# Attention, gating mixer and feed-forward on one core: norms placed earlier, root by Newton steps, one split per weight pair

## The chip, the core and the metric

One core of a Trainium2 chip runs the whole program. The metric is device time in microseconds, the median of several executions. Four engines matter here: TensorE (PE) does the matmuls, VectorE (DVE) and ScalarE (ACT) the elementwise work, and SyncE's queue (SP) issues the DMAs. Each executes its instructions in order.

## The reference

Three layers follow one another on 4 sequences of 576 tokens with 512 features, in fp32:

```
attn:  8 heads of 64; heads 0-3 see the last 32 positions, heads 4-7 every 32nd earlier one
h = gelu_tanh(x @ w_in);  u, v = h[:, :512], h[:, 512:]
v_n = (v - mean(v)) / sqrt(var(v) + 1e-6) * g_ln
x   = x + (u * (w_sg @ v_n + b_sg)) @ w_out          # w_sg mixes the 576 tokens
xn  = (x - mean(x)) / sqrt(var(x) + 1e-6) * g_2
out = x + relu(xn @ w_ch1) @ w_ch2                   # 512 -> 2048 -> 512
```

## The kernel before

**Numbers.** A matmul runs in a reduced fp32 format, so every operand is split into a high part (a cast on ACT) and a low part (the difference, on DVE), and every product is three matmuls: low x high, high x low, high x high (`split` L177, `mm3` L202). Some weights arrive as 64-bit floats and are first turned into fp32 by one ACT and two DVE operations (`from_f64` L186).

**First three stages, batch by batch.** For each of the four sequences there are segments v (5 token tiles, then gelu and norm of v), u (8 groups), g (8 groups, the gate) and y (8 groups, output and residual). The attention of the next sequence is placed between the groups of the one before. Each finished row block y goes to DRAM (`y_d`). Hooks put extra work in front of a group: `PREP_AT`, `NORM0_AT` and `PRE_AT` are lists of such places.

**Last stage.** The 2304 tokens are taken in three blocks of 768 (`sc` 0, 1, 2), each as two halves of 384. The first matrix (512 -> 2048) is computed in 8 pairs of 128-column blocks (`pair` L829) by a scheme with 7 block products in place of 8: each product is 6 matmuls, 42 per pair. It needs 7 combinations of the tokens, x0 to x6 (`expand` L751), and 7 combinations of each weight pair (`combine` L634). The results of the second half, `late`, are kept, while the first half goes on into the second matrix (`ch2` L796): 24 matmuls per pair for the pair before. After 8 pairs the second half is done, 12 matmuls for each of 16 blocks, and `leave` (L818) multiplies by the reciprocal root of the variance, adds the residual and stores.

**Weights.** While block 0 runs, the weights of later pairs are prepared: `piece` loads (and converts) a quarter, `combine` forms three further differences and splits them, `second` splits the second matrix's part. `units` lists these steps, and `prepare(n)` does the next n. Some pieces (`PRE`) are converted in earlier batches and kept in DRAM. `keep` stores a finished pair in DRAM, `fetch` loads it again for blocks 1 and 2. Two buffers hold the first matrix's pairs in turn.

**Norm of a block.** `norm` (L711) has six steps: load; mean of half 0 and of half 1 (`col_sum` adds the four feature blocks on DVE and splits, two matmuls with a matrix of ones add over partitions, one DVE operation subtracts); variance of half 0 and half 1 (squares on ACT, adds on DVE, split, two matmuls); then the scale by g on ACT. `rsqrt` (L741) makes the reciprocal root, needed only in `leave`. Within one step the sum and the matmuls that use it follow one another. For block 0 `NORM0_AT` puts the steps into segments g and y of the last batch; for block 1 the steps come after pairs 6 and 7 of block 0, for block 2 after pairs 2 to 7 of block 1 (`NORM_AT` L65). For blocks 1 and 2, the two scratch tiles of `col_sum`, those of `rsqrt` and the result tile of `leave` share one name, o, with two buffers.

**Order.** The written order is a priority. A planner with its own cost figures goes through the program, gives each engine the first instruction whose inputs are ready by those figures, and fixes each engine's order. Memory is given out in pools on two stacks; a pool's tile can be written only when what lay there before is done. `open_a` to `open_d` (L935 to L966) open the last stage's pools at the last batch's v 0, g 0, y 0 and after it.

Of the kernel before, what the change touches and what calls it, by code (L numbers as in the profile page):

```python
# [43 lines left out]
WX = {1: (0, 0), 2: (1, 1), 7: (2, 5), 4: (3, 2), 5: (4, 3), 6: (5, 4), 3: (6, 6)}  # L44
S_ENGINE = lambda nc: nc.vector
# [103 lines left out]
def mixer_kernel(ctx: ExitStack, tc: tile.TileContext, io, out):  # L149
# [484 lines left out]
    def combine(i):  # L634
        stg = big["stg"]
        wf = stg[:, 2048:3072].bitcast(F32).rearrange("p (k f) -> p k f", k=KD)
        s = stg[:, 4096:4864].bitcast(F32).rearrange("p (s k f) -> p s k f", s=3, k=2)
        a11, a21, a12, a22 = wf[:, 0:2, 0:P], wf[:, 0:2, P:2 * P], wf[:, 2:4, 0:P], wf[:, 2:4, P:2 * P]
        tt = S_ENGINE(nc).tensor_tensor
# [4 lines left out]
        w = w1[i] = big["w1", i % 2].tile([P, 2, 7, 2, P], F32R, tag="w1", name=f"w1_{i % 2}")  # L644
        for src, j, m in ((wf[:, :, 0:P], 0, 2), (wf[:, :, P:2 * P], 2, 2), (s.rearrange("p s k f -> p (s k) f"), 4, 3)):
            split(w[:, 0, j:j + m].rearrange("p s k f -> p (s k) f"), w[:, 1, j:j + m].rearrange("p s k f -> p (s k) f"),
                  src)

    def keep(i):
        nc.sync.dma_start(out=w1_d[i], in_=w1[i].rearrange("p a s k f -> p (a s k f)").bitcast(F32))  # L650

    def fetch(i):
        w = w1[i] = big["w1", i % 2].tile([P, 2, 7, 2, P], F32R, tag="w1", name=f"w1_{i % 2}")
        nc.sync.dma_start(out=w.rearrange("p a s k f -> p (a s k f)").bitcast(F32), in_=w1_d[i])

    def second(i):
        f = big["stg"][:, 3072:4096].bitcast(F32)
# [52 lines left out]

    def norm(sc, step, role):  # L711
# [6 lines left out]
        if step in (1, 2):  # L718
            half = step - 1
            cs = slice(half * TH, (half + 1) * TH)  # L720
            sr = col_sum(sc, half, False)
            mean = bank(role, "ps_m")[:, :TH]
            nc.tensor.matmul(mean, lhsT=one, rhs=sr[:, 1, :], start=True, stop=False)
            nc.tensor.matmul(mean, lhsT=one, rhs=sr[:, 0, :], start=False, stop=True)
            nc.vector.scalar_tensor_tensor(
                out=yc[:, :, cs], in0=mean.unsqueeze(1).to_broadcast([P, KD, TH]), scalar=-1.0 / DM,
                in1=yc[:, :, cs], op0=ALU.mult, op1=ALU.add)
        elif step in (3, 4):
            half = step - 3
            sr = col_sum(sc, half, True)  # L730
            o = bank(role, "ps_v2")[:, :TH]
            nc.tensor.matmul(o, lhsT=one, rhs=sr[:, 1, :], start=True, stop=False)
            nc.tensor.matmul(o, lhsT=one, rhs=sr[:, 0, :], start=False, stop=True)
            if half == 0:
                rbs[sc] = big["rb"].tile([P, 2, TH], F32, tag="rb", name="rb", bufs=2)
            nc.scalar.activation(rbs[sc][:, half, :], o, AF.Identity, scale=1.0 / DM, bias=eps)
        else:
            for k in range(KD):
                nc.scalar.activation(yc[:, k, :], yc[:, k, :], AF.Copy, scale=g_2[:, k:k + 1])

    def rsqrt(sc, half):  # L741
        ve = rbs[sc][:, half, :]
        t, r = scratch(1, 0), scratch(1, 1)
# [4 lines left out]
        nc.vector.tensor_scalar(out=t, in0=t, scalar1=-0.5, scalar2=1.5, op0=ALU.mult, op1=ALU.add)
        nc.vector.tensor_tensor(out=ve, in0=r, in1=t, op=ALU.mult)

    def expand(sc, step):  # L751
# [7 lines left out]
        if step == 0:
            put(0, b11)  # L760
            tt(out=b11, in0=b12, in1=b11, op=ALU.subtract)
        elif step == 1:
            put(6, b22)
            tt(out=b12, in0=b22, in1=b12, op=ALU.subtract)
        elif step == 2:
            tt(out=b22, in0=b22, in1=b11, op=ALU.subtract)
            put(4, b22)
        elif step == 3:
            put(1, b21)
            tt(out=b21, in0=b22, in1=b21, op=ALU.subtract)  # L770
        elif step == 4:
            put(5, b12)
        elif step == 5:
            put(2, b21)
        else:
            put(3, b11)
# [158 lines left out]
    def open_a():  # L935
        close("at")
        right("wst")
        right(("w1", 0))
        big["stg"] = big["wst"].tile([P, 4864], U32, tag="stg", name="stg")

    def open_b():
        close("win")
        right(("w1", 1))
        right(("w2", 0))
# [73 lines left out]
```

## Time and profile before

| | us |
|---|---|
| median of 3 runs | 697.91 (697.89 to 699.45) |
| the profiled execution | 699.26 |
| its span | 697.5 |
| PE busy | 672.5 (96%) |
| DVE busy | 474.0 (68%) |
| ACT busy | 319.0 (46%) |
| mean granted clock of PE | 0.985 |

The page gives busy time per engine and, in 40 slices, how busy each was. The views used below list one engine's instructions in order of time, with the idle time before one and what ended it, or the busy time of every engine in a stretch. The last stage's matmuls begin at 298.7 us.

### The profile page before, as it was taken

How to read it: one execution, taken by the hardware profiler on the slowest of the kernel's cores; microseconds unless marked ns; L12 is line 12 of the kernel's file. 1: busy time of each engine (PE TensorE's matmuls, PEld its weight loads, DVE VectorE, ACT ScalarE, POOL GpSimd, SP SyncE). 2: the span in 40 equal slices, each digit the busy share in tenths (PEclk: the TensorE clock that was granted, in tenths of full speed). 3: DMA queues.
4: the chain of work that ended last, by engine and by line, in shares of the span. 5: the costliest groups of instructions: out<-in, count | busy, mean ns of one | idle time of the engine just before them, and what ended most of it. 6: DMA issues, size and time to landing. Idle time of an engine off the chain costs nothing.

```text
span 697.5 us, 12744 instructions
## 1 busy us (share of the span) xinstructions
PE 672.5 (96%) x5050; PEld 642.9 (92%) x5050; DVE 474.0 (68%) x992; ACT 319.0 (46%) x803; POOL 21.0 (3%) x24
## 2 busy tenths in 40 slices
PE   5899999999999999989999969999999999999997
PEld 4779979989898989979999969999999999999997
DVE  4889787586758685999998885644679347333433
ACT  3888967283568445655454553112434222111121
POOL 0011011000200020000000000000000000000000
PEclk9899999999999999999999979999999999999999
DMA  8863233457431565337867714354335415353001
GB/s 267 274 188 126 84 98 111 150 161 220 150 110 47 194 223 178 125 136 281 306 243 260 283 45 136 92 209 168 151 129 220 149 57 209 121 209 108 22 25 45
DMA packets 34539, 110.05 MB, mean 158 GB/s; under 512 B 3696, under 2 KB 13936, under 8 KB 31408
## 3 DMA queue, kind: packets, MB, share of 16 engines
q1 hardware_dynamic: 34480, 109.25, 46.1%
q8 instruction: 39, 0.64, 0.4%
q14 instruction: 20, 0.16, 0.1%
HBM read 82.76 MB, written 26.48 MB: 157 GB/s over the span
## 4 chain that ended last, share of the span: by engine, by line
PE 75%; DVE 10%; ACT 8%; DMA 5%; issue 1%; SPq 1%; ACTq 0%; DVEq 0%
PE ps_p L783 21%; PE ps_o L205 9%; PE ps_o L204 8%; PE ps_o L203 8%; PE ps_u L203 2%; PE ps_u L205 2%; PE ps_u L204 2%; PE ps_v L203 2%; PE ps_v L204 2%; PE ps_v L205 2%; PE ps_y L203 2%; PE ps_y L205 2%; PE ps_y L204 2%; ACT pt L400 2%; PE ps_t L439 1%
## 5 line engine op out<-in xcount | busy, mean ns | idle before, releaser
L783 PE MATMUL ps_p<-x,w 128*128 128x384 f32 x1008 | 188.2, 339 | 6.2 <-DVE o L821 3.1
L783 PEld LDWEIGHTS ps_p<-x,w 128*128 128x128 f32 x1008 | 177.3, 190 | 9.4 <-DVE o L821 3.4
L204 PE MATMUL ps_o<-h,w 128*128 128x384 f32 x384 | 129.7, 338 | 0.0
L205 PE MATMUL ps_o<-h,w 128*128 128x384 f32 x384 | 129.4, 338 | 0.0
L203 PE MATMUL ps_o<-h,w 128*128 128x384 f32 x384 | 128.6, 336 | 0.0
L205 PEld LDWEIGHTS ps_o<-h,w 128*128 128x128 f32 x384 | 73.3, 191 | 0.0
L204 PEld LDWEIGHTS ps_o<-h,w 128*128 128x128 f32 x384 | 73.1, 190 | 0.1
L203 PEld LDWEIGHTS ps_o<-h,w 128*128 128x128 f32 x384 | 72.6, 189 | 0.2
L789 DVE SCALAR_TENSOR_TENSOR h<-late,h 128x384 fp32r<-128x384 f32 x48 | 26.5, 558 | 47.4 <-ACT h L788 47.4
L788 ACT ACTIVATE h<-late 128x384 fp32r<-128x384 f32 x48 | 25.2, 525 | 68.0 <-PE ps_o L205 68.0
L203 PE MATMUL ps_g<-wsg,vn 128*128 128x288 f32 x128 | 39.0, 305 | 0.0
L205 PE MATMUL ps_g<-wsg,vn 128*128 128x288 f32 x128 | 38.2, 299 | 0.0
L203 PE MATMUL ps_u<-xhl,winl 128*128 128x288 f32 x128 | 38.1, 297 | 0.0
L203 PE MATMUL ps_y<-gt,wout 128*128 128x288 f32 x128 | 37.9, 298 | 0.0
L204 PE MATMUL ps_g<-wsg,vn 128*128 128x288 f32 x128 | 37.9, 296 | 0.0
L204 PE MATMUL ps_u<-xhl,winh 128*128 128x288 f32 x128 | 37.8, 295 | 0.0
L205 PE MATMUL ps_u<-xhl,winh 128*128 128x288 f32 x128 | 37.7, 295 | 0.0
L205 PE MATMUL ps_y<-gt,wout 128*128 128x288 f32 x128 | 37.6, 295 | 0.0
L204 PE MATMUL ps_y<-gt,wout 128*128 128x288 f32 x128 | 37.5, 294 | 0.0
L788 ACT ACTIVATE h<-c 128x384 fp32r<-128x384 f32 x24 | 12.6, 523 | 51.4 <-DVE c L851 51.3
L835 ACT ACTIVATE s<-ps_p 128x384 f32<-128x384 f32 x24 | 11.7, 489 | 49.7 <-PE ps_p L783 49.6
L203 PE MATMUL ps_v<-winh,xhl 128*128 128x512 f32 x80 | 32.2, 403 | 0.2 <-DVE xhl L495 0.2
(183 smaller groups left out, 1328.0 us busy)
## 6 DMA issues: line engine op xcount, KB each, us to landing
w<-w_scratch SPq DMA_DIRECT2D x16, 1792.0 KB, 7.4
w_scratch<-w SPq DMA_DIRECT2D x8, 1792.0 KB, 7.3
stg<-in_w_ch SPq DMA_DIRECT2D x23, 512.0 KB, 5.9
qk<-in_qk_s SPq DMA_DIRECT2D x8, 601.0 KB, 4.3
raw_p<-in_w_ch SPq DMA_DIRECT2D x18, 256.0 KB, 3.1
y_scratch<-y SPq DMA_DIRECT2D x16, 288.0 KB, 2.8
yc<-y_scratch SPq DMA_DIRECT2D x3, 1536.0 KB, 6.9
qk<-in_qk_l SPq DMA_DIRECT2D x7, 592.0 KB, 5.0
```

Of the source, the lines that this page charges most:

```text
L203: nc.tensor.matmul(ps, lhsT=ll, rhs=rh, start=first, stop=False)
L204: nc.tensor.matmul(ps, lhsT=lh, rhs=rl, start=False, stop=False)
L205: last_mm[0] = nc.tensor.matmul(ps, lhsT=lh, rhs=rh, start=False, stop=last)
L400: exps.append(nc.scalar.activation(p3[:, i, :], src, AF.Exp, scale=SCALE, bias=mx[:, i:i + 1], accum_out=sm[:, i:i + 1]))
L439: nc.tensor.transpose(ps[:rows, (t - t0) * c:(t - t0 + 1) * c], src, ident)
L783: nc.tensor.matmul(o, lhsT=w[:, a, wj, k, :], rhs=x[:, c, k, :], start=first and k == 0 and n == 0, stop=k == 1 and n == 2, skip_group_che ...
L788: nc.scalar.activation(h[:, 0, :], src, AF.Relu)
L789: nc.vector.scalar_tensor_tensor(out=h[:, 1, :], in0=src, scalar=0.0, in1=h[:, 0, :], op0=ALU.max, op1=ALU.subtract)
L835: nc.scalar.activation(s1, a, AF.Copy)
```

## The change

The first block's norm moves from the last batch's g and y segments into v and u, its expansion into g and y; the memory for it is opened at v 0 and that of the first weight pair later, at g 0. Each norm step now ends with the column sum of the next step, whose matmuls come one step later; steps for block 1 go after pairs 3 to 6 of block 0 and into the middle of pairs (4.5, 5.5, 6.5). The root starts from ACT's Abs_reciprocal_sqrt and takes two Newton steps in place of Sqrt, reciprocal and one step. A weight pair's 14 blocks lie side by side and are split in one operation each on ACT and DVE. The list of weight steps is reordered, one more piece is converted early, and 13 of the steps instead of 12 are done ahead of the last stage.

```
-PREP_AT = (("u", 2, 2), ("u", 6, 1), ("g", 2, 2), ("g", 4, 1), ("g", 5, 2), ("y", 2, 1), ("y", 4, 2), ("y", 6, 1))
-NORM0_AT = (("g", 0, "n", 0), ("g", 3, "n", 1), ("g", 4, "n", 2), ("g", 6, "n", 3), ("g", 7, "n", 4), ("y", 1, "n", 5),
-            ("y", 2, "e", 0), ("y", 2, "e", 1), ("y", 3, "e", 2), ("y", 4, "e", 3), ("y", 5, "e", 4), ("y", 6, "e", 5),
-            ("y", 7, "e", 6))
-NORM_AT = ({6: (0, 1), 7: (2, 3, 4, 5)}, {2: (0,), 3: (1,), 4: (2,), 5: (3,), 6: (4,), 7: (5,)})
+PREP_AT = (("v", 1, 1), ("v", 3, 1), ("u", 2, 1), ("u", 4, 1), ("g", 1, 1), ("g", 2, 1), ("g", 3, 1), ("g", 4, 1),
+           ("y", 2, 1), ("y", 6, 1), ("y", 7, 1))
+NORM0_AT = (("v", 0, "n", 0), ("v", 4, "n", 1), ("u", 2, "n", 2), ("u", 4, "n", 3), ("u", 6, "n", 4), ("g", 0, "n", 5),
+            ("g", 5, "e", 0), ("g", 7, "e", 1), ("y", 0, "e", 2), ("y", 1, "e", 3), ("y", 2, "e", 4), ("y", 3, "e", 5),
+            ("y", 5, "e", 6))
+NORM_AT = ({3: (0,), 4.5: (1,), 5: (2,), 5.5: (3,), 6: (4,), 6.5: (5,)}, {2: (0,), 3: (1,), 4: (2,), 5: (3,), 6: (4,), 6.5: (5,)})
-PRE = (8, 9, 12, 13, 16, 17, 20, 21, 24)
+PRE = (8, 9, 12, 13, 16, 17, 20, 21, 24, 25)
...
     def combine(i):
         stg = big["stg"]
...
+        c = stg[:, 3072:4864].bitcast(F32)
...
-        for src, j, m in ((wf[:, :, 0:P], 0, 2), (wf[:, :, P:2 * P], 2, 2), (s.rearrange("p s k f -> p (s k) f"), 4, 3)):
-            split(w[:, 0, j:j + m].rearrange("p s k f -> p (s k) f"), w[:, 1, j:j + m].rearrange("p s k f -> p (s k) f"),
-                  src)
+        split(w[:, 0].rearrange("p n f -> p (n f)"), w[:, 1].rearrange("p n f -> p (n f)"), c)
...
-    units = [(fn, a) for i in range(NW) for fn, a in (
-        (piece, (i, 0)), (piece, (i, 1)), (combine, (i,)), (piece, (i, 2)), (piece, (i, 3)), (second, (i,)))]
+    units = [(piece, (0, 0)), (piece, (0, 1)), (piece, (0, 2)), (piece, (0, 3)), (combine, (0,))]
+    for i in range(NW):
+        if i:
+            units += [(piece, (i, 2)), (piece, (i, 3))]
+        if i + 1 < NW:
+            units += [(piece, (i + 1, 0)), (piece, (i + 1, 1))]
+        units += [(second, (i,))]
+        if i + 1 < NW:
+            units += [(combine, (i + 1,))]
...
+        if 1 < step < 6:
+            half = step % 2
             cs = slice(half * TH, (half + 1) * TH)
+            sr = srs.pop(sc)
+            o = bank(role, "ps_m")[:, :TH]
             nc.tensor.matmul(o, lhsT=one, rhs=sr[:, 1, :], start=True, stop=False)
             nc.tensor.matmul(o, lhsT=one, rhs=sr[:, 0, :], start=False, stop=True)
+            if step < 4:
+                nc.vector.scalar_tensor_tensor(
+                    out=yc[:, :, cs], in0=o.unsqueeze(1).to_broadcast([P, KD, TH]), scalar=-1.0 / DM,
+                    in1=yc[:, :, cs], op0=ALU.mult, op1=ALU.add)
+            else:
+                if half == 0:
+                    rbs[sc] = big["rb"].tile([P, 2, TH], F32, tag="rb", name="rb", bufs=2)
+                nc.scalar.activation(rbs[sc][:, half, :], o, AF.Identity, scale=1.0 / DM, bias=eps)
+        if step < 5:
+            srs[sc] = col_sum(sc, (step - 1) % 2, step > 2)
         else:
             for k in range(KD):
                 nc.scalar.activation(yc[:, k, :], yc[:, k, :], AF.Copy, scale=g_2[:, k:k + 1])
...
-        nc.scalar.activation(t, ve, AF.Sqrt)
-        nc.vector.reciprocal(r, t)
-        nc.scalar.activation(t, r, AF.Square)
-        nc.vector.tensor_tensor(out=t, in0=t, in1=ve, op=ALU.mult)
-        nc.vector.tensor_scalar(out=t, in0=t, scalar1=-0.5, scalar2=1.5, op0=ALU.mult, op1=ALU.add)
-        nc.vector.tensor_tensor(out=ve, in0=r, in1=t, op=ALU.mult)
+        nc.scalar.activation(r, ve, AF.Abs_reciprocal_sqrt)
+        for step in range(2):
+            nc.scalar.activation(t, r, AF.Square)
+            nc.vector.tensor_tensor(out=t, in0=t, in1=ve, op=ALU.mult)
+            nc.vector.tensor_scalar(out=t, in0=t, scalar1=-0.5, scalar2=1.5, op0=ALU.mult, op1=ALU.add)
+            nc.vector.tensor_tensor(out=ve if step else r, in0=r, in1=t, op=ALU.mult)
...
+        what = ((0, "t1", 6, "t3"), ("t2", 4), (1, "t4"), (5,), (2,), (3,), ())
+        if sc == 0:
+            what = ((0, "t1"), ("t2", 4), (1, "t4"), ("t3", 5), (2,), (3,), (6,))
...
         if i:
             ch2(sc, 0, f1 - 2, 1 - role)
+        mid()                      # norm steps of i - 0.5
         e = bank(role, "ps_p4")[:, :TH]
...
     def open_a():
         close("at")
         right("wst")
-        right(("w1", 0))
+        right("nm")
+        right("sr")
+        right("rb")
+        big["norm", 0] = big["nm"].tile([P, KD * TC + 2 * TH], F32, tag="n0", name="n0")
         big["stg"] = big["wst"].tile([P, 4864], U32, tag="stg", name="stg")
     def open_b():
         close("win")
+        right(("w1", 0))
         right(("w1", 1))
         right(("w2", 0))
-        right(("w2", 1))
...
+        right(("x", 0))            # x0 and x4
     def open_c():
         close("mid")
-        right("x")
+        right(("x", 1))            # the other five
+        right(("w2", 1))
         right(("w2", 2))
...
-    prepare(max(0, 12 - done[0]))
+    prepare(max(0, 13 - done[0]))
```

## Rows read from the trace of the kernel before

**Rows 1.** The page: busy time of the engines, and the group of products.
```profile
PE 672.5 (96%) x5050; PEld 642.9 (92%) x5050; DVE 474.0 (68%) x992; ACT 319.0 (46%) x803; POOL 21.0 (3%) x24
L783 PE MATMUL ps_p<-x,w 128*128 128x384 f32 x1008 | 188.2, 339 | 6.2 <-DVE o L821 3.1
```
**Rows 2.** Windows: stretch, length, busy time by engine, PE clock, DMA share, GB/s.
```profile
240.00:298.70 58.70, 58.34 (x394) 55.64 (x393) 46.62 (x95) 33.09 (x61) 6.22 (x5) 1.00 0.53 190
298.70:308.50 9.80, 7.60 (x33) 6.26 (x31) 9.80 (x15) 6.22 (x10) 0.00 (x0) 0.83 0.05 16
308.50:396.50 88.00, 87.65 (x501) 86.85 (x502) 81.45 (x150) 41.81 (x71) 0.00 (x0) 1.00 0.78 274
396.50:418.30 21.80, 15.67 (x63) 13.98 (x62) 17.01 (x26) 14.80 (x25) 0.00 (x0) 0.77 0.27 104
510.00:545.00 35.00, 35.00 (x203) 34.91 (x202) 31.38 (x48) 13.81 (x23) 0.00 (x0) 1.00 0.52 186
298.70:690.36 391.66, 382.98 (x2162) 378.79 (x2161) 245.88 (x428) 128.82 (x228) 0.00 (x0) 0.98 0.44 157
```
**Rows 3.** The chain that ended last: 30 undisturbed matmuls (start, length).
```profile
333.31 5.20 PE ps_p L783 x30
```
**Rows 4.** PE's timeline at the stage's head: start, length, instruction, idle before.
```profile
300.42 0.45 PE L783 MATMUL ps_p<-x,w 128*128 128x384 f32 x1 [0.51 <-ACT x L179]
302.02 5.94 PE L783 MATMUL ps_p<-x,w 128*128 128x384 f32 x23 [1.16 <-ACT x L179]
```
**Rows 5.** PE's timeline at the change from block 0 to block 1.
```profile
397.61 0.45 PE L732 MATMUL ps_v<-sr,one 128*128 128x384 f32 x1 [0.74 <-DVE sr L180]
...
403.21 0.44 PE L732 MATMUL ps_v<-sr,one 128*128 128x384 f32 x1 [1.75 <-DVE sr L180]
...
412.34 2.29 PE L783 MATMUL ps_p<-x,w 128*128 128x384 f32 x6 [3.06 <-DVE o L821]
415.21 0.69 PE L783 MATMUL ps_p<-x,w 128*128 128x384 f32 x1 [0.58 <-ACT s L835]
```
**Rows 6.** Timelines of DVE and of SP's queue at the head.
```profile
299.27 0.96 DVE L180 TENSOR_TENSOR x<-n,x 128x768 fp32r<-128x768 f32 x1
300.14 0.95 DVE L766 TENSOR_TENSOR n<-n 128x768 f32<-128x768 f32 x1
...
297.10 10.56 SPq L590 DMA_DIRECT2D y_scratch<-y  x2
```
**Rows 7.** DVE's timeline at the change from block 0 to block 1.
```profile
403.83 2.55 DVE L745 RECIPROCAL o<-o 128x384 f32<-128x384 f32 x1 [0.68 <-ACT o L744]
...
410.39 0.56 DVE L749 TENSOR_TENSOR rb<-o 128x384 f32<-128x384 f32 x1
...
411.73 1.02 DVE L821 TENSOR_TENSOR o<-ps_o,rb 128x384 f32<-128x384 f32 x2
```
**Rows 8.** Timelines of SP's queue and of PE in the last batch.
```profile
246.00 12.54 SPq L188 DMA_DIRECT2D stg<-in_w_ch  x4
269.16 0.38 SPq L715 DMA_DIRECT2D n<-y_scratch  x1
...
279.43 0.44 PE L723 MATMUL ps_m<-sr,one 128*128 128x384 f32 x1 [0.36 <-DVE sr L180]
```
**Rows 9.** DVE: one row of its timeline, then groups (count, busy, mean ns).
```profile
358.02 0.55 DVE L704 TENSOR_TENSOR o<-yc 128x384 f32<-128x384 f32 x1
...
L180 DVE TENSOR_TENSOR w<-stg,w 128x512 fp32r<-128x512 f32 x16 | 10.6, 686 | 0.1
L180 DVE TENSOR_TENSOR w<-stg,w 128x1024 fp32r<-128x1024 f32 x8 | 9.7, 1215 | 6.5 <-ACT w L179 6.5
L748 DVE TENSOR_SCALAR o<-o 128x384 f32<-128x384 f32 x6 | 2.1, 356 | 0.1
```
**Rows 10.** ACT's timeline: the root's table load, and a square.
```profile
323.66 1.28 ACT L744 ACT_TABLE_LOAD   x1
...
282.87 0.51 ACT L701 ACTIVATE n<-n 128x384 f32<-128x384 f32 x1
```

More of the change, by code (lines that the diff above doesn't have):

```diff
@@ L43 @@
 NLATE = 10
[L44 to L45 removed]
+WX = {1: (0, 2, 0), 2: (4, 2, 1), 7: (1, 2, 5), 4: (5, 2, 2), 5: (8, 1, 3), 6: (10, 1, 4), 3: (12, 1, 6)}
 NT = B * S
@@ L623, in piece @@
         stg = big["stg"]
-        w0 = 2048 + 1024 * (j // 2) + WP * (j % 2)
+        w0 = 2048 + 1024 * (1 - j // 2) + WP * (j % 2)
         w = stg[:, w0:w0 + WP]
@@ L635, in combine @@
         stg = big["stg"]
-        wf = stg[:, 2048:3072].bitcast(F32).rearrange("p (k f) -> p k f", k=KD)
-        s = stg[:, 4096:4864].bitcast(F32).rearrange("p (s k f) -> p s k f", s=3, k=2)
+        c = stg[:, 3072:4864].bitcast(F32)
+        wf = c[:, 0:1024].rearrange("p (k f) -> p k f", k=KD)
+        s = c[:, 1024:1792].rearrange("p (s k f) -> p s k f", s=3, k=2)
         a11, a21, a12, a22 = wf[:, 0:2, 0:P], wf[:, 0:2, P:2 * P], wf[:, 2:4, 0:P], wf[:, 2:4, P:2 * P]
-        tt = S_ENGINE(nc).tensor_tensor
+        tt = nc.vector.tensor_tensor
         tt(out=s[:, 0], in0=a21, in1=a22, op=ALU.add)
@@ L643, in combine @@
         tt(out=s[:, 2], in0=a12, in1=s[:, 1], op=ALU.subtract)
[L644 to L647 removed]
+        w = w1[i] = big["w1", i % 2].tile([P, 2, 14, P], F32R, tag="w1", name=f"w1_{i % 2}")
+        split(w[:, 0].rearrange("p n f -> p (n f)"), w[:, 1].rearrange("p n f -> p (n f)"), c)
     def keep(i):
[L650 removed]
+        nc.sync.dma_start(out=w1_d[i], in_=w1[i].rearrange("p a n f -> p (a n f)").bitcast(F32))
     def fetch(i):
[L653 to L654 removed]
+        w = w1[i] = big["w1", i % 2].tile([P, 2, 14, P], F32R, tag="w1", name=f"w1_{i % 2}")
+        nc.sync.dma_start(out=w.rearrange("p a n f -> p (a n f)").bitcast(F32), in_=w1_d[i])
     def second(i):
[L657 removed]
+        f = big["stg"][:, 2048:3072].bitcast(F32)
         w = w2[i] = big["w2", i].tile([P, 2, 2, DM], F32R, name=f"w2_{i}")
         split(w[:, 0].rearrange("p k f -> p (k f)"), w[:, 1].rearrange("p k f -> p (k f)"), f)
[L661 to L662 removed]
+    units = [(piece, (0, 0)), (piece, (0, 1)), (piece, (0, 2)), (piece, (0, 3)), (combine, (0,))]
[7 more added lines that the diff above has]
+            units += [(combine, (i + 1,))]
     done = [0]
@@ L709, in col_sum @@
         return sr
+    srs = {}
     def norm(sc, step, role):
@@ L717, in norm @@
         yc = ys[sc]
-        if step in (1, 2):
-            half = step - 1
+        if 1 < step < 6:
+            half = step % 2
             cs = slice(half * TH, (half + 1) * TH)
[L721 to L731, printed above, removed]
+            sr = srs.pop(sc)
+            o = bank(role, "ps_m")[:, :TH]
             nc.tensor.matmul(o, lhsT=one, rhs=sr[:, 1, :], start=True, stop=False)
             nc.tensor.matmul(o, lhsT=one, rhs=sr[:, 0, :], start=False, stop=True)
-            if half == 0:
-                rbs[sc] = big["rb"].tile([P, 2, TH], F32, tag="rb", name="rb", bufs=2)
-            nc.scalar.activation(rbs[sc][:, half, :], o, AF.Identity, scale=1.0 / DM, bias=eps)
+            if step < 4:
[8 more added lines that the diff above has]
+            srs[sc] = col_sum(sc, (step - 1) % 2, step > 2)
         else:
@@ L756, in put @@
         def put(j, src):
-            x = xns[sc, j] = big["x"].tile([P, 2, 2, TH], F32R, tag=f"x{j}", name=f"x{j}")
+            pl = big["x", 0 if j in (0, 4) else 1]
+            x = xns[sc, j] = pl.tile([P, 2, 2, TH], F32R, tag=f"x{j}", name=f"x{j}")
             split(x[:, 0], x[:, 1], src)
[L759 to L776, printed above, removed]
+        t2 = b22 if sc else big["norm", 0][:, KD * TC:].rearrange("p (k t) -> p k t", k=2)
+        what = ((0, "t1", 6, "t3"), ("t2", 4), (1, "t4"), (5,), (2,), (3,), ())
+        if sc == 0:
+            what = ((0, "t1"), ("t2", 4), (1, "t4"), ("t3", 5), (2,), (3,), (6,))
+        for w in what[step]:
+            if w == "t1":
+                tt(out=b11, in0=b12, in1=b11, op=ALU.subtract)
+            elif w == "t2":
+                tt(out=t2, in0=b22, in1=b11, op=ALU.subtract)
+            elif w == "t3":
+                tt(out=b12, in0=b22, in1=b12, op=ALU.subtract)
+            elif w == "t4":
+                tt(out=b21, in0=t2, in1=b21, op=ALU.subtract)
+            else:
+                put(w, {0: b11, 1: b21, 2: b21, 3: b11, 4: t2, 5: b12, 6: b22}[w])
     def product(sc, i, o, m, first):
-        wj, xj = WX[m]
+        n0, nk, xj = WX[m]
         w, x = w1[i], xns[sc, xj]
@@ L782, in product @@
             for n, (a, c) in enumerate(((1, 0), (0, 1), (0, 0))):
-                nc.tensor.matmul(o, lhsT=w[:, a, wj, k, :], rhs=x[:, c, k, :], start=first and k == 0 and n == 0,
+                nc.tensor.matmul(o, lhsT=w[:, a, n0 + nk * k, :], rhs=x[:, c, k, :], start=first and k == 0 and n == 0,
                                  stop=k == 1 and n == 2, skip_group_check=True)
@@ L827, in tmp, with pair @@
         return big["tmp"].tile([P, TH], F32, tag=tag, name=tag, bufs=2 if tag == "u2" else 1)
-    def pair(sc, i, role):
+    def pair(sc, i, role, mid):
         tt = nc.vector.tensor_tensor
@@ L860, in pair, with steps_at @@
         hs[f1], hs[f2] = h1, h2
+    def steps_at(sc, i, role):
+        if sc + 1 < NSC:
+            for step in NORM_AT[sc > 0].get(i, ()):
+                norm(sc + 1, step, role)
     def last_stage():
@@ L865, in last_stage @@
             for i in range(NW):
-                pair(sc, i, role)
+                pair(sc, i, role, lambda: steps_at(sc, i - 0.5, role))
                 if sc == 0:
@@ L873, in last_stage @@
                     fetch(i + 2)
-                if sc + 1 < NSC:
-                    for step in NORM_AT[sc > 0].get(i, ()):
-                        norm(sc + 1, step, role)
+                steps_at(sc, i, role)
                 if i == NW - 3:
@@ L937, in open_a @@
         right("wst")
-        right(("w1", 0))
[L939 to L944, printed above, removed]
-        right(("w2", 1))
         right("nm")
@@ L949, in open_b @@
         big["norm", 0] = big["nm"].tile([P, KD * TC + 2 * TH], F32, tag="n0", name="n0")
+        big["stg"] = big["wst"].tile([P, 4864], U32, tag="stg", name="stg")
+    def open_b():
+        close("win")
+        right(("w1", 0))
+        right(("w1", 1))
+        right(("w2", 0))
+        right(("x", 0))
     def open_c():
         close("mid")
-        right("x")
+        right(("x", 1))
+        right(("w2", 1))
         right(("w2", 2))
```

8 lines of the change are left out of this document (4 added, 4 removed).

## The prediction

> **What bounds the kernel now.** The page first: PE is busy 672.5 of 697.5 us, VectorE (DVE) 474, ScalarE (ACT) 319, so the time is PE's matmuls plus what PE loses between them [rows 1]. Stretches second: the last stage runs from 298.7 to 690.36, and PE's clock falls in two places of it, to 0.83 and 0.77 on average [rows 2]. The stage's matmuls: 1008 products [rows 1] and, by the code, 3 x 2 x 16 x 12 = 1152 of the second matrix and 16 for column sums, 2176 in all. Undisturbed, 30 take 5.20 us, 0.1733 each [rows 3], so 2176 need 377.1; the stage takes 391.66 [rows 2]. **PE loses 14.5 us there**, and that is my ceiling. (The trace holds 2162 records; 14 are missing, so I count by the program.)
>
> PE's own timeline shows where. At the head, from 299.91 (the 0.51 wait before 300.42) to 308.5, only 24 matmuls run, 4.2 us of 8.6: 4.4 lost, to waits for the normed tiles x and then to a slow clock [rows 2, 4]. At the change from the first 768 tokens to the second, 396.5 to 418.3, PE waits 0.74 and 1.75 for column sums, 3.06 for a DVE result at L821 and 0.58 for ACT, 6.1 together [rows 5]; the other 3.9 of the remaining 10 us is the clock at 0.77 (six matmuls take 2.29 there) [rows 2, 5]. Between them, 308.5 to 396.5, PE is busy 87.65 of 88.0 although DVE is busy 81.45, 93% [rows 2]. The second change, 510 to 545, where the norm is spread over pairs 2 to 7 and no weights are prepared, loses nothing: PE 35.0 of 35.0 [rows 2].
>
> The cause at the head is DVE: 9.8 busy of 9.8 us, filled with the expansion of the first tokens (five splits, three differences) [rows 2, 6]. SP's queue is in order too: a y store waits there until 307.7 and no weight load passes it [rows 6]; DMA is at 0.05 [rows 2]. The cause at the change is a chain through the two buffers named o, which column sums, the root and `leave` share: the last sum reaches PE at 403.21 [rows 5], the root's RECIPROCAL takes 2.55 from 403.83, its last product is at 410.39, and only then L821 at 411.73 frees PE's bank [rows 7].
>
> **Part 1: first norm and expansion move ahead of the stage.** The 1536 KB load n is issued at 269.16, when the u stage has freed its memory [rows 8]. The change lets it go at the v stage; on SP it can stand behind four weight loads, issued over 12.54 us from 246.0 [rows 8], so at worst it goes at 258.5, 10.7 us earlier. All its instructions come along: column sums with 8 matmuls, squares, scaling. What crosses from after 298.7 to before it are eight DVE operations of 0.87 us in line (0.96 long, the next starts 0.87 later, so 0.09 overlap) [rows 6], 7.0 us, with the ACT halves of the five splits. DVE has 58.7 less 46.62 = 12.1 us idle in 240 to 298.7 [rows 2]; 7.0 fit, leaving 91% load. The y stage alone gets crowded: five of the seven x tiles can be written only when the gating stage's memory is free, but 42 products (7.3 us) need them one after the other, x6 last. Gain 4.4; I leave 0.5 of it for a late x. If the cover is gone, the 7.0 stand again in front of PE and nothing is won at the head.
>
> New waits: the first weight pair's tile now opens after u, so its split goes to about 270; behind it on ACT and DVE stand the gate's z and gt, while PE wants the weights only at 298.7. The sum matmuls move into u, and PE executes in order, so a late sum holds the u matmuls behind it. Of twelve such sums now three wait, 0.36, 0.74 and 1.75 [rows 5, 8]; ends for the eight moved ones: nothing, and 8 x 1.75 = 14.0. I take 0.5 in all, nearest to the 0.36 in the gating stage, since a sum's matmuls now stand a whole step (two u groups or half a pair) behind its split.
>
> **Part 2: the second norm spreads over pairs 3 to 6.5.** It removes the waits on sums and the o chain: the last column sum is started after pair 6, and both roots can end before `leave`, in the order that the second change already has. The question is DVE in the first pairs. Its work from 298.7 to 396.5 is 9.8 + 81.45 = 91.25 us [rows 2]. Less the expansion, 7.0; less two h splits of the next half (0.56 - 0.09 = 0.47 each, the length of L749 [rows 7]), 0.9; plus three adds and two sum splits that now come earlier, 2.3; roots: one now (2.46 + 0.47 + 0.27 + 0.47 = 3.7), two afterwards, each with two Newton steps of 0.47 + 0.27 + 0.47, 4.8 together [rows 7, 9], so plus 1.1; less one conversion, two operations on 512 columns, under 1.2 by the 512 row, 0.9 taken; less 0.8 for merged splits (part 4): 85.0. PE needs 42 matmuls for pair 0, 7 x 66 and 24 more, 528 x 0.1733 = 91.5 us. That is 93%, what DVE carries now between 308.5 and 396.5 while PE loses 0.35 [rows 2]. I take 1.0 for the pairs and 0.5 at the change. If DVE fails there, see the second rival.
>
> **Part 3: root by Newton steps.** RECIPROCAL goes; an extra step costs one ACT square and three DVE operations, counted above. The new ACT function is not in the trace: between nothing and a square's 0.51 plus a table load of 1.28 for each of six halves, 10.7 on ACT [rows 10]; I take 0.51 and one load in all, as the Sqrt pays now. ACT is busy 6.2 + 41.8 = 48.0 of 97.8 there [rows 2], which hides it; uncovered, at most 1.8 per half.
>
> The row shows one load at the root and none before a square at 282.87, after Gelu [rows 10]. The Trainium skill, "ScalarE: Activation LUTs", section "Table sets: the hidden batching unit", says that every function outside the active set costs a load. By that rule a root whose set lacks its neighbours would load twice per half, an estimated 12 x 1.28 = 15.4 us of ACT over three token blocks. The trace shows no such case; ACT's idle half would hide most, and the sum would stay.
>
> **Part 4: one split per weight pair, one more piece converted early, new order of pieces.** Three DVE splits (512, 512 and 768 columns: 0.69 + 0.69 + 0.95 along the rows' slope of 0.53 per 512, less 0.09 each, 2.06) become one of 1792 columns, which no row shows: between 1.2 (the 1024 row) and 2.3 (the three summed); along the slope 2.01, in line 1.92 [rows 9]. That is 0.14 x 6 = 0.8. The extra piece (two loads, conversions and stores) lies in batch 2's u stage beside matmuls: nothing, and uncovered about the conversion's 0.9. Order of pieces: nothing either way.
>
> **Sum.** 14.5 - 0.5 - 0.5 - 1.0 - 0.5 = 12.0 us. The profiled execution took 699.26 (span 697.5 and 1.76 around it), so 687.3; that run was 1.35 over the median of three, 697.91, so for a median **685.9**, say 686. The 7.1 us of DVE work after PE's last matmul stay.
>
> Another ceiling: LDWEIGHTS is busy 378.79 of 391.66 [rows 2], 12.9 idle. The Trainium skill, "Perfetto Trace Analysis", section "Identifying the Most-Contended Engine", judges PE's headroom by that row and not by matmul busy time. By it the same subtractions give 687.5; by the pace of matmuls 685.9. Loads at the slow clock count as busy there, which is why I keep the pace.
>
> **Rivals.** (1) Forecast, 686, own range 683.5 to 689.5: 0.60. (2) DVE becomes the bound in pairs 4 to 7: the mean's subtraction, one long instruction, stands in order ahead of the c21, h2 and u that PE waits for. Four pairs at 1.3 each: 5.2 less gain, 691. For it: 93% load. Against: the same load now costs 0.35. 0.18. (3) The change does not do what it says: the written places are priorities for a planner, which already pulled a sum of the second norm to 358 [rows 9] though it is written at pair 7. If the o chain stays last, only the head is won: 697.9 - 4.4 = 693.5. Against: the second change keeps the order. 0.06. (4) Slower: the moved sums stall PE where it runs without a gap today, the u stage and the pairs. Eight at the worst row, 14.0, and at the change 6.1 us of waits brought 3.9 of slow clock, 0.64 per us, so 9.0 more: 697.9 - 14.5 + 23.0 = 706.4. It decides from 14.5 / (8 x 1.64) = 1.1 us a sum. For it: 1.75 was seen. Against: nine of twelve wait not at all. 0.12, of which 0.04 lands near no change. (5) Nothing new stalls, and small waits ahead of the stage vanish too: 682.5. 0.04.
>
> **Numbers.** A measurement here tells about 0.3% (2.1 us) from no change. Faster: (1), (2), (3), (5), 0.88; same 0.04; slower 0.08. The range holds (1), (2) and half of (5): 682.5 to 692.5.
>
> **What would show it.** Part 1: n's load before 260, the 0.87 us splits over before 299, products at 0.173 from the first, clock 1.0. Part 2: the second norm's sums between pairs 4 and 7, no L821 wait of PE, DVE near 93% in the first pairs with PE above 99%. Part 3: no RECIPROCAL, one table load. Wrong: PE waiting on sums in the u stage for more than 1 us each, or products waiting for u, c21 or weights in pairs 4 to 7.

## Result, and the profile after

The kernel after takes 687.19 us (median of 4 runs, 686.18 to 688.23), the kernel before beside it 698.17 (697.89 to 699.45): a ratio of 0.9839, 95% interval 0.9818 to 0.9861, so 11.2 us faster, give or take 1.5. The profiled execution took 686.18 with a span of 684.4; by the profiled runs the gain is 13.1, because that of before lay 1.1 above its median and that of after 1.0 below.

The page of the kernel after, to be held against [rows 1]: DVE's share is still 68%, PE's busy time fell by 8.8 us (it runs at the slow clock less), and products wait 1.3 us in place of 6.2.
```profile
PE 663.7 (97%) x5050; PEld 635.6 (93%) x5050; DVE 466.2 (68%) x990; ACT 318.9 (47%) x794; POOL 19.6 (3%) x24
...
L788 PE MATMUL ps_p<-x,w 128*128 128x384 f32 x1008 | 184.1, 335 | 1.3 <-DVE u L844 1.1
```
Windows of the kernel after (stretch, length, then PE, PEld, DVE, ACT, POOL busy, PE clock, DMA share, GB/s), as [rows 2]. The last stage's first product now starts at 296.55 in place of 298.71, so the stretches are shifted by 2 us. This is no gain by itself: 24 matmuls of the y stage now come behind its first 11 products, up to 301.6. The granted clock is 1.00 in each; at the change from the first to the second 768 tokens (388.5 to 410) PE works 21.46 of 21.5 us. In the pairs before it DVE is busy 77.05 of 82 us, 94%, and PE 99.7%.
```profile
240.00:296.70 56.70, 55.65 (x370) 52.65 (x369) 47.45 (x88) 35.49 (x61) 4.62 (x5) 1.00 0.32 109
296.70:306.50 9.80, 8.66 (x56) 8.35 (x55) 9.38 (x19) 2.96 (x3) 0.00 (x0) 1.00 0.48 189
306.50:388.50 82.00, 81.76 (x466) 80.27 (x465) 77.05 (x134) 44.71 (x67) 0.00 (x0) 1.00 0.80 297
388.50:410.00 21.50, 21.46 (x123) 21.37 (x124) 21.28 (x40) 13.95 (x25) 0.00 (x0) 1.00 0.43 169
```
All that PE waits for in the kernel after from 240 us to 690 (us in total, times, longest). Of the waits of [rows 5] none is left; the two that matter are u at the head of the last stage and a sum, in the u stage.
```profile
PE ps_p L788 <- DVE u L844: 1.1, 1, 1.1
PE ps_m L731 <- DVE sr L180: 1.0, 1, 1.0
PE ps_p L788 <- DVE h L794: 0.2, 1, 0.2
```
DVE at the change in the kernel after (start, length), as [rows 7]: the last column sum's split ends at 389.4, where before its matmul waited until 403.21. The two roots end with the rb rows at 397.87 and 404.76, in pieces of 0.36 to 0.56 between other work, and only then comes `leave` (L826): the o chain no longer holds PE's banks when PE needs them.
```profile
388.87 0.55 DVE L180 TENSOR_TENSOR sr<-o,sr 128x384 fp32r<-128x384 f32 x1
...
397.87 0.55 DVE L755 TENSOR_TENSOR rb<-o 128x384 f32<-128x384 f32 x1
...
404.76 0.55 DVE L755 TENSOR_TENSOR rb<-o 128x384 f32<-128x384 f32 x1
...
406.10 1.01 DVE L826 TENSOR_TENSOR o<-ps_o,rb 128x384 f32<-128x384 f32 x2
```

To compare kernels by stretch I count, from each trace's matmul records, the time from one start to the next less the pace of its shape (0.173 us for 384 columns as in [rows 3], 0.133 for 288, 0.217 for 512), and sum it; the rounded paces leave some 0.2 of doubt in a column. Each row is one profiled execution, which can lie off its kernel's median (most in e5, 700.07 against 697.21). Ratios are to the kernel before beside each, with the 95% interval; that of e10 leaves out one execution of 817.89 us at a granted clock of 0.75.

This count does not agree with the ceiling of the prediction. PE's matmuls do not end at 690.36 but at 693.28, and no record is missing: the trace holds all 2176, 16 of them after 690.36. Windows of before and of after over the whole stage:
```profile
298.70:693.28 394.58, 385.90 (x2178) 381.55 (x2176) 248.70 (x433) 128.82 (x228) 0.00 (x0) 0.98 0.44 156
296.55:680.00 383.45, 382.04 (x2202) 379.78 (x2200) 240.07 (x437) 127.52 (x217) 0.00 (x0) 1.00 0.47 171
```
Before, 394.6 less 377.1 (2176 x 0.1733) are 17.5 us of loss, not 14.5. After, 24 matmuls of the y stage (3.2 us) lie within, so 3.2 of loss are left there: 14.3 won inside the stage.

| PE's loss, us | ahead, 232-298 | head, 298-310 | pairs, 310-390 | change, 390-430 | ratio |
|---|---|---|---|---|---|
| before | 1.4 | 4.8 | 1.0 | 11.4 | 1 |
| after | 2.5 | 1.7 | 1.3 | 0.05 | 0.9839 (0.9818-0.9861) |
| e1 after, second norm late | 4.6 | 1.4 | 0.5 | 9.6 | 0.9978 (0.9964-0.9991) |
| e2 before, second norm spread | 1.5 | 4.8 | 1.4 | 1.0 | 0.9862 (0.9847-0.9877) |
| e3 before, `leave` without o | 1.4 | 4.8 | 2.4 | 9.0 | 0.9958 (0.9940-0.9976) |
| e4 after, old root | 3.1 | 1.8 | 1.1 | 4.7 | 0.9910 (0.9895-0.9925) |
| e5 after, sums not a step ahead | 3.3 | 0.8 | 1.9 | 11.1 | 0.9960 (0.9943-0.9977) |
| e6 after, first norm late | 2.5 | 4.1 | 2.3 | 0.5 | 0.9858 (0.9828-0.9888) |
| e7 after, two mends | 3.0 | 0.04 | 2.4 | 0.5 | 0.9817 (0.9793-0.9841) |
| e8 after, old root, norm earlier | 4.7 | 2.0 | 3.9 | 5.2 | 0.9932 (0.9905-0.9958) |
| e9 after, three splits | 5.1 | 1.6 | 6.6 | 1.5 | 0.9942 (0.9920-0.9965) |
| e10 e2 with the new root | 1.2 | 4.8 | 1.6 | 0.01 | 0.9838 (0.9812-0.9864) |
| e11 after, four steps later | 2.9 | 1.1 | 1.2 | 1.2 | 0.9834 (0.9812-0.9855) |

So in the profiled runs the change gained 11.35, the head 3.1, the pairs gave 0.3 back and the stages ahead 1.1.

### The profile page after: what moved, and what is told of

Read it like the earlier page. It is cut to its first block, busy times and chain, and to the rows that moved or that the text cites. A ratio compares the mean times of both kernels' runs of the same rounds, so it can differ in the third digit from the quotient of the medians.

```text
span 684.4 us, 12749 instructions
## 1 busy us (share of the span) xinstructions
PE 663.7 (97%) x5050; PEld 635.6 (93%) x5050; DVE 466.2 (68%) x990; ACT 318.9 (47%) x794; POOL 19.6 (3%) x24
## 4 chain that ended last, share of the span: by engine, by line
PE 69%; DVE 10%; DMA 8%; ACT 8%; issue 2%; SPq 1%; POOL 1%; DVEq 0%; ACTq 0%; POOLq 0%
PE ps_p L788 24%; PE ps_o L204 10%; PE ps_o L205 10%; PE ps_o L203 9%; DMA w_scratch<-w_p 3%; ACT pt L400 2%; DMA qk<-in_qk_l 2%; PE ps_g L203 1%; PE ps_pv L458 1%; DMA y_scratch<-y 1%; PE ps_g L205 1%; DMA n<-y_scratch 1%; PE ps_g L204 1%; PE ps_t L439 1%; ACT pts L400 1%
## 5 line engine op out<-in xcount | busy, mean ns | idle before, releaser
L788 PE MATMUL ps_p<-x,w 128*128 128x384 f32 x1008 | 184.1, 335 | 1.3 <-DVE u L844 1.1
L788 PEld LDWEIGHTS ps_p<-x,w 128*128 128x128 f32 x1008 | 175.0, 188 | 3.0 <-DVE u L844 1.5
L205 PE MATMUL ps_o<-h,w 128*128 128x384 f32 x384 | 128.3, 334 | 0.0
L204 PE MATMUL ps_o<-h,w 128*128 128x384 f32 x384 | 128.3, 334 | 0.0
L203 PE MATMUL ps_o<-h,w 128*128 128x384 f32 x384 | 126.8, 334 | 0.1
L203 PEld LDWEIGHTS ps_o<-h,w 128*128 128x128 f32 x384 | 71.9, 188 | 0.4 <-ACT h L793 0.4
L204 PEld LDWEIGHTS ps_o<-h,w 128*128 128x128 f32 x384 | 72.1, 188 | 0.1
L205 PEld LDWEIGHTS ps_o<-h,w 128*128 128x128 f32 x384 | 72.1, 188 | 0.0
```

What stands on the lines that cost most here:

```text
L203: nc.tensor.matmul(ps, lhsT=ll, rhs=rh, start=first, stop=False)
L204: nc.tensor.matmul(ps, lhsT=lh, rhs=rl, start=False, stop=False)
L205: last_mm[0] = nc.tensor.matmul(ps, lhsT=lh, rhs=rh, start=False, stop=last)
L788: nc.tensor.matmul(o, lhsT=w[:, a, n0 + nk * k, :], rhs=x[:, c, k, :], start=first and k == 0 and n == 0, stop=k == 1 and n == 2, skip_gro ...
```

## Experiments

**e1: the second norm put back to pairs 6 and 7.**
```
-NORM_AT = ({3: (0,), 4.5: (1,), 5: (2,), 5.5: (3,), 6: (4,), 6.5: (5,)}, {2: (0,), ...
+NORM_AT = ({6: (0, 1), 7: (2, 3, 4, 5)}, {2: (0,), ...
```


> The changed kernel with only block 1's norm put back after pairs 6 and 7 of block 0. Theory A (the gain is mostly the change from block 0 to block 1: waits for column sums and the chain through the two o buffers): PE loses about 10 us there again, 695 to 698 us. Rival B (the gain comes from the earlier first norm and from less DVE work): at most 3 us of it goes, 687 to 690 us.

0.9978 against after's 0.9839: 0.0139 x 698 = 9.7 us of the gain go, as theory A expected. The loss at the change is 9.6 again; 2.1 more are lost ahead of the stage, where a sum's matmul waits 2.0, and 1.1 less in head and pairs. PE's timeline of e1 (idle before and its releaser in brackets) shows a wait for a sum back at the change, longer than any in [rows 5].
```profile
401.69 0.69 PE L731 MATMUL ps_m<-sr,one 128*128 128x384 f32 x1 [3.97 <-DVE sr L180]
```

**e2: the spread alone, in the kernel before.**
```
-NORM_AT = ({6: (0, 1), 7: (2, 3, 4, 5)}, {2: (0,), ...
+NORM_AT = ({2: (0,), 3: (1,), 4: (2,), 5: (3,), 6: (4,), 7: (5,)}, {2: (0,), ...
```


> The kernel before with only block 1's norm steps spread over pairs 2 to 7 of block 0, sums and their matmuls still in one step, old root, old splits. Theory A: about 10 us come from this alone, 687 to 690 us. Rival B (DVE at 93% has no room without the other savings, so PE waits inside the pairs instead): 692 to 699 us.

0.9862: one edited line of the kernel before wins 9.6 us of the 11.2. DVE's timeline of e2: the last sum is split 17 us earlier than before, both RECIPROCALs come before the change, and `leave` (L821) at 400.71 stands 11 us ahead of [rows 7].
```profile
385.64 0.55 DVE L180 TENSOR_TENSOR sr<-o,sr 128x384 fp32r<-128x384 f32 x1
...
393.96 2.54 DVE L745 RECIPROCAL o<-o 128x384 f32<-128x384 f32 x1
...
400.71 1.01 DVE L821 TENSOR_TENSOR o<-ps_o,rb 128x384 f32<-128x384 f32 x2
```

**e3: `leave` writes its product back into PE's bank, so it needs no o buffer** (kernel before; same work).
```
-        r = big["tmp"].tile([P, TH], F32, tag="o", name="o", bufs=2)
+        r = accs[half, d][:, :TH]
```


> The kernel before, but leave writes its product back into the PSUM bank, so it needs no o buffer. Theory A (the o buffers hold leave behind the root): the 3.1 us wait of PE for L821 and the slow clock after it go, 692 to 695 us. Rival C (leave is late only because DVE's queue ahead of it is full): the wait stays, 697 to 699 us.

0.9958, a gain of 2.9 us, just short of what theory A expected. The 3.06 us wait for L821 is gone: `leave` starts at 396.64 in place of 411.73 (DVE's timeline of e3), so the two o buffers were indeed what held it.
```profile
396.64 0.56 DVE L821 TENSOR_TENSOR ps_o<-ps_o,rb 128x384 f32<-128x384 f32 x1
```
But the loss at the change falls only from 11.4 to 9.0. PE's timeline of e3 shows longer waits for sums than the 0.74 and 1.75 of before: the late sums remain when the chain is cut behind them.
```profile
399.11 0.44 PE L732 MATMUL ps_v<-sr,one 128*128 128x384 f32 x1 [1.46 <-DVE sr L180]
...
408.02 0.69 PE L732 MATMUL ps_v<-sr,one 128*128 128x384 f32 x1 [3.24 <-DVE sr L180]
```

**e4: the old root (Sqrt, RECIPROCAL, one Newton step) in the kernel after.**
```
-        nc.scalar.activation(r, ve, AF.Abs_reciprocal_sqrt)
-        for step in range(2):
+        nc.scalar.activation(t, ve, AF.Sqrt)
+        nc.vector.reciprocal(r, t)
...
```


> The changed kernel with the old root (Sqrt, RECIPROCAL of 2.55 us, one Newton step). Theory A: the root is hidden once the norm is spread, within 0.7 us of the changed kernel, 686 to 688.5 us. Rival B (the saved 1.3 us of DVE per half counts in pairs 6 and 7): 689 us or more, with PE waits on DVE in these pairs.

Theory A expected no difference; it came out 0.0071 x 698 = 5.0 us slower than the kernel after, which is the time of rival B, though the wait falls at the change and not in pairs 6 and 7. PE's timeline of e4 first, then DVE's: half 1's RECIPROCAL, 2.55 us, stands directly ahead of the h split that PE's next matmul needs, and PE waits 2.55. The slow clock follows: the window of e4 has a granted clock of 0.67, and wait and clock together make the 4.7 of loss at the change.
```profile
402.88 0.45 PE L204 MATMUL ps_o<-h,w 128*128 128x384 f32 x1 [2.55 <-DVE h L794]
```
```profile
399.87 2.55 DVE L751 RECIPROCAL o<-o 128x384 f32<-128x384 f32 x1 [0.16 <-ACT o L750]
402.34 0.49 DVE L794 SCALAR_TENSOR_TENSOR h<-late,h 128x384 fp32r<-128x384 f32 x1
```
```profile
402.80:408.00 5.20, 5.12 (x20) 5.12 (x21) 5.20 (x11) 1.55 (x3) 0.00 (x0) 0.67 0.10 44
```

**e5: each column sum in the step of its own matmuls again** (kernel after).
```
-            sr = srs.pop(sc)
+            sr = col_sum(sc, half, step > 3)
...
-        if step < 5:
-            srs[sc] = col_sum(sc, (step - 1) % 2, step > 2)
-        else:
+        if step == 5:
```


> The changed kernel with every column sum put back into the step of its own matmuls, all places as changed. Theory A (the gap of a step between a sum and its matmuls hides it): PE waits at several of the eight sums, 0.4 to 1.8 us each, 689 to 693 us. Rival D (the planner pulls the sums ahead anyway, so where they are written matters little): within 1 us of the changed kernel.

0.9960, 8.4 us over the kernel after and worse than expected. DVE's timeline of e5, then PE's: at after's places, half a pair apart, the sums without their lead end at 400.7 in place of 389.4. The root's pieces, the expansion and `leave` (L824, 411.25 against 406.10) crowd behind them, and the h operation on which PE waits 3.31 comes only at 408.70, among these.
```profile
400.11 0.56 DVE L180 TENSOR_TENSOR sr<-o,sr 128x384 fp32r<-128x384 f32 x1 [0.68 <-ACT sr L179]
...
408.70 0.55 DVE L792 SCALAR_TENSOR_TENSOR h<-late,h 128x384 fp32r<-128x384 f32 x1
...
411.25 1.01 DVE L824 TENSOR_TENSOR o<-ps_o,rb 128x384 f32<-128x384 f32 x2
```
```profile
409.31 0.69 PE L204 MATMUL ps_o<-h,w 128*128 128x384 f32 x1 [3.31 <-DVE h L792]
```

**e6: the first norm and expansion, with their memory, at before's places** (kernel after): `NORM0_AT` as before; n, sr, rb and x open where they did.


> The changed kernel with block 1's spread, new root and merged splits kept, but block 0's norm and expansion back at their old places and memory (norm tile opened after u). Theory A: the head loses about 3 us more and the u stage 1.3 us less, 688 to 690 us. Rival B (the earlier first norm is the main part): 693 us or more.

0.9858, in the expected range and 1.3 us over the kernel after, but with intervals of 2.1 and 1.5 us to either side the two are not told apart. The head loses 4.1 again. The 1.3 us that the u stage was to give back did not come: ahead of the stage e6 loses 2.5, as much as the kernel after, now with PE's waits of 0.6 in the u stage and 0.3 in the y stage for operations of these stages.

**e7: two mends of the kernel after**: three norm steps one u or g group later, no weight steps in y 6 and y 7.
```
-           ("y", 2, 1), ("y", 6, 1), ("y", 7, 1))
+           ("y", 2, 1))
-NORM0_AT = (... ("u", 4, "n", 3), ("u", 6, "n", 4), ("g", 0, "n", 5),
+NORM0_AT = (... ("u", 5, "n", 3), ("u", 7, "n", 4), ("g", 1, "n", 5),
...
-                        prepare(len(units[done[0]:]) if i + 3 == NW else 6)
+                        prepare(len(units[done[0]:]) if i + 3 == NW else 6 if i else 10)
...
-    prepare(max(0, 13 - done[0]))
+    prepare(max(0, 9 - done[0]))
```


> The changed kernel with the third to sixth norm step of block 0 written one u group later (u 5, u 7, g 1) and the last two weight pieces ahead of the stage left to pair 0. Theory A (the 1.2 us wait of a u group for the second column sum and the 1.1 us wait of a product for u behind the pieces' conversions are all that is left to mend there): both waits go, 684.5 to 686 us. Rival: the waits move to the next sum and to the weights of pair 2, no gain, 687 us or more.

0.9817 (0.9793 to 0.9841): not told apart from the kernel after. The head's loss went to 0.04, but the wait for a sum did not leave; it moved to a later sum, still among the matmuls of u (1.32 us at 272.61), and the pairs lose 1.1 more.

**e8: the old root with the second norm's steps earlier** (kernel after with e4's root).
```
-NORM_AT = ({3: (0,), 4.5: (1,), 5: (2,), 5.5: (3,), 6: (4,), 6.5: (5,)}, {2: (0,), ...
+NORM_AT = ({2: (0,), 3: (1,), 3.5: (2,), 4: (3,), 5: (4,), 6: (5,)}, {2: (0,), ...
```


> The changed kernel with the old root, and block 1's norm steps one to one and a half pairs earlier (2, 3, 3.5, 4, 5, 6). Theory E (the old root costs 5 us only because it falls into the h operations after pair 7, where its RECIPROCAL stands ahead of an h that PE waits for; earlier it falls beside pair 6): 686.5 to 689 us. Rival F (2.5 us of RECIPROCAL hurts wherever it is): 691 us or more.

0.9932, no better than the 0.9910 of e4: earlier places do not save the old root here. DVE's timeline of e8, then PE's: now half 0's RECIPROCAL stands ahead of a weight split, and products wait 1.35 for that.
```profile
385.38 2.54 DVE L751 RECIPROCAL o<-o 128x384 f32<-128x384 f32 x1
387.84 1.96 DVE L180 TENSOR_TENSOR w<-stg,w 128x1792 fp32r<-128x1792 f32 x1
```
```profile
389.85 5.47 PE L788 MATMUL ps_p<-x,w 128*128 128x384 f32 x30 [1.35 <-DVE w L180]
```
The earlier places with the new root were not run, so what the places cost by themselves is open; ahead of the stage e8 loses 2.2 more than the kernel after, with a wait of 2.0 for a sum in place of 1.05.

**e9: three splits per weight pair again** (kernel after).
```
-        split(w[:, 0].rearrange("p n f -> p (n f)"), w[:, 1].rearrange("p n f -> p (n f)"), c)
+        for j, m in ((0, 4), (4, 4), (8, 6)):
+            split(w[:, 0, j:j + m].rearrange("p n f -> p (n f)"), w[:, 1, j:j + m].rearrange("p n f -> p (n f)"),
+                  c[:, j * P:(j + m) * P])
```


> The kernel after, but a weight pair's 14 blocks are split in three operations of 512, 512 and 768 columns on ACT and on DVE, as before the change. Theory (the prediction's part 4): six pairs cost DVE 0.14 us more each, 0.8 in all, and it lies in DVE's gaps: the time stays within 1 us of the kernel after (ratio to the kernel before 0.983 to 0.986). Rival G: with DVE at 95% in the pairs nothing is free, 0.8 to 2 us more (0.985 to 0.987). Rival H: the one long split of 2.0 us holds up what stands behind it on DVE as RECIPROCAL did; then three short ones are faster by 1 us or more (below 0.9825).

0.9942, 0.0103 x 698 = 7.2 us slower than the kernel after: outside every expectation, with only 1.9 us more of DVE. The table puts 5.3 of it into the pairs, 2.6 ahead of the stage (one wait for a sum, 2.5 against 1.05 in the kernel after) and 1.4 at the change. ACT, DVE and PE of e9 soon after the head, one after the other: the planner, given other operations, puts the second matrix's split ahead of s on ACT, where it waits 6.37 us for a conversion; then a y addition that waits for a DMA goes ahead of u on DVE, and PE waits 1.28 and 2.39 us. The 12 products after the second wait run at 0.35 each, at a granted clock of 0.50.
```profile
308.39 1.06 ACT L179 ACTIVATE w<-stg 128x1024 fp32r<-128x1024 f32 x1 [6.37 <-DVE stg L196]
309.35 0.47 ACT L842 ACTIVATE s<-ps_p 128x384 f32<-128x384 f32 x1
```
```profile
311.66 0.82 DVE L588 TENSOR_TENSOR y<-ps_y,x 128x288 f32<-128x288 f32 x2 [0.70 <-DMA y_scratch<-y]
312.40 0.55 DVE L846 TENSOR_TENSOR u<-ps_p,s 128x384 f32<-128x384 f32 x1
```
```profile
309.88 1.33 PE L790 MATMUL ps_p<-x,w 128*128 128x384 f32 x6 [1.28 <-ACT s L842]
313.60 4.21 PE L790 MATMUL ps_p<-x,w 128*128 128x384 f32 x12 [2.39 <-DVE u L852]
```
```profile
313.60:317.80 4.20, 4.20 (x12) 3.70 (x12) 3.14 (x7) 2.05 (x4) 0.00 (x0) 0.50 0.87 278
```
Whether one long or three short splits matter in themselves would need both in the same order of instructions; that was not run.

**e10: e2 and the new root** (kernel before with the two edits alone; three splits, first norm late).


> The kernel before with the second norm's steps after pairs 2 to 7 (as in e2) and the root by Abs_reciprocal_sqrt and two Newton steps. The root was worth 5 us in the kernel after (e4) . Theory E (RECIPROCAL costs where an operation that PE needs stands right behind it): e2 lost 0.97 us at the change and 1.38 in the pairs, so the new root can win back no more than that: 686.5 to 688.5, 0.3 to 2 us under e2 (ratio 0.983 to 0.986). Rival I (the root's worth is DVE's load, not its place): it wins some 5 us here too, 684 (below 0.981). Rival J (the root alone does nothing where the sums end early): the same as e2, 0.986 to 0.988.

0.9838 (0.9812 to 0.9864): level with the kernel after, with two of its parts alone. The loss at the change goes from 1.0 to 0.01; against e2 the time falls by 1.7 us, with intervals that overlap. Windows of e10: PE is without a gap at the change, though DVE is busy 97% in the pairs and 97% there.
```profile
306.50:388.50 82.00, 81.37 (x464) 79.75 (x463) 79.26 (x150) 50.22 (x83) 0.00 (x0) 1.00 0.77 280
388.50:410.00 21.50, 21.50 (x126) 21.45 (x125) 20.93 (x41) 10.47 (x19) 0.00 (x0) 1.00 0.44 162
```

**e11: four weight steps later** (the weight half of e7's edit).


> The kernel after with four weight steps fewer ahead of the last stage (9 in place of 13, none in front of y groups 6 and 7) and four more after pair 0. Theory: the wait of 1.14 us for u at the stage's head stands behind weight conversions on DVE; without them the head's loss of 1.7 us goes and the time falls by 1 to 1.7 us against the kernel after (ratio 0.981 to 0.9825). Rival: DVE at 95% in the pairs has no room for four steps more, and what the head wins is lost in pairs 1 to 3: no difference (0.983 to 0.986).

0.9834, no difference, as the rival expected, but not in the place that it named. The head gained 0.6; pairs 1 to 3 lost nothing, and the change lost 1.2: the last sum's split comes 1.8 us later than in the kernel after, at 390.71 against 388.87.

## Why the prediction was right, and where its steps were not

**The cause held; the size of the ceiling did not.** That the last column sum is late, and that root and `leave` queue behind it, is shown from both sides by e1 and e2 (9.7 and 9.6 us); e3 shows that the o chain alone is the smaller part (2.9). The second rival (DVE bound in the pairs, 691) fails: 94% by the windows, 93% predicted, and PE at 99.7%; e10 carries 97%.

But I ended the stage at 690.36, some 3 us too early, and took the records behind it for missing. PE lost 17.5 us in the stage and not 14.5, 11.4 of them at the change and not 10.0; of these the part beside the waits of 6.1 was 5.3 and not 3.9. (For the same reason 4 us follow PE's last matmul, not 7.1.) With 17.5 my subtractions would have come to 682.9, below the forecast's own range. They were too small as well: the stage kept 3.2 of loss where I left 2.0 (head 1.7 for 0.5, pairs 1.25 for 1.0, change 0.05 for 0.5, after it 0.15 for nothing), and ahead of it 1.1 went where I left 0.5. 17.5 - 3.2 - 1.1 = 13.2 is the profiled gain of 13.1. So the forecast came as near as it did because two errors, 3.0 and 1.8, were opposite; that much is luck.

**Part 1 was sized too high.** The n load went at 228.6, before the 260 that I asked for, but the last x split still came at 301.27, with the last matmuls of the y stage, not before 299. The head kept 1.7 us of loss where 0.5 was left. DVE's timeline of the kernel after: u, on which PE waits 1.14, stands behind a 2.02 us weight split, that x split and two weight conversions (the split itself was estimated at 2.01).
```profile
299.34 2.02 DVE L180 TENSOR_TENSOR w<-stg,w 128x1792 fp32r<-128x1792 f32 x1
301.27 0.96 DVE L180 TENSOR_TENSOR x<-n,x 128x768 fp32r<-128x768 f32 x1
...
305.03 0.68 DVE L196 SCALAR_TENSOR_TENSOR stg<-stg 128x512 uint32<-128x512 uint32 x1
305.63 0.55 DVE L844 TENSOR_TENSOR u<-ps_p,s 128x384 f32<-128x384 f32 x1
```
And one of the moved sums made PE wait 1.05, from start to start a loss of 1.2, where 0.5 was left for all. It is the mechanism of the slower rival, but once and not eight times. ACT's timeline of the kernel after shows why: in order, the sum's cast stands behind a value norm that waits for GpSimd.
```profile
261.37 0.72 ACT L522 ACTIVATE vn<-g,rs 128x512 fp32r<-128x512 f32 x1 [1.88 <-POOL rs L519]
...
262.81 0.51 ACT L179 ACTIVATE sr<-n 128x384 fp32r<-128x384 f32 x1
```
Of 3.4 us predicted for head and sums (4.4 less 0.5 and 0.5), the trace shows 3.1 less 1.1, so 2.0. The times do not show this part: e6 without it is 1.3 us slower, within the noise, and no better ahead of the stage; e10 without it is level.

**Parts 3 and 4 failed as single terms.** I priced the root and the merged split by the DVE time they add or remove (about 1 us each) and held them hidden. Taken out of the kernel after, they cost 5.0 (e4) and 7.2 us (e9). The price was the place: a 2.55 us instruction in an in-order queue delays whatever PE needs next behind it, and each edit makes the planner order all engines anew. Against another order they are worth little: e2 has the old root and three splits and is 1.6 us from the kernel after, e10 has three splits and is level with it. So these prices do not add up. The kernels that lose at most 1.2 at the change (after, e2, e6, e7, e10, e11) all end between 0.982 and 0.986, with 5.5 to 9.4 us of loss left in the four columns; of the others, all but e9, which loses most in the pairs, lose 4.7 or more there and end at 0.991 or above.

**The other signs.** There is no RECIPROCAL in the root, no wait of PE for `leave`, and one table load for six roots, as the trace of the kernel after shows on ACT:
```profile
388.61 1.28 ACT L750 ACT_TABLE_LOAD   x1
389.90 0.53 ACT L750 ACTIVATE o<-rb 128x384 f32<-128x384 f32 x1
```
By the rule of the Trainium skill, "ScalarE: Activation LUTs", section "Table sets: the hidden batching unit", that a function from another set needs a load, up to twelve could have come; the trace shows that this function's neighbours needed none of their own. The other ceiling, idle LDWEIGHTS, was too low: over the whole stage these are idle 394.58 less 381.55, 13.0 us, and 14.3 were won there.

**Open.** After, e7, e10 and e11 keep 5.5 to 7.6 us of loss in different places and end level. A ratio is good to some 1.6 us, so which of these losses still costs time was not settled; nor was a second scratch buffer for the sums tried.

## What to carry to other kernels

Where a block of work ends in a chain over a shared small buffer, look at when the chain's first link starts before shortening the chain: starting the norm's steps earlier was worth 9.6 us, taking `leave` off the shared buffer 2.9. Price an operation on an in-order engine by what stands behind it at its place, not by its share of the engine's busy time. In a kernel whose order a planner makes, take an edit out and also put it alone into the old kernel, since the two can differ by several us.

## What the runs showed of the hardware

RECIPROCAL on 384 columns takes 2.55 us where a tensor_tensor takes 0.55; with the next instruction starting 2.46 and 0.47 later, that is 5.2 times. The Trainium skill, "VectorE: DVE Perf Modes", section "First, the fixed hardware budget", says it is an iterated division repeated 8 times; the rows agree that it is long, by less than 8. Single waits of 1.05 and 1.14 us in the kernel after left the granted clock at 1.00 in the 3 us behind them. In e4 a single wait of 2.55 us was followed by a granted clock of 0.67 over the next 5 us, and in e9, after 1.28 and 2.39 us close together, 12 products ran at 0.35 us at a granted clock of 0.50, the lower level of 1.2 GHz.
